# Reordering the first 28 slots of a fused thresholded attention and MoE kernel: scores first, copies a slot later, maxima two slots ahead of the gate

## The chip, the cores and the metric

The kernel runs on one core of a Trainium2 chip. A core has four compute engines with queues of their own: TensorE (PE, matmuls), VectorE (DVE), ScalarE (ACT) and GpSimd (POOL). A fifth, SyncE (SP), issues most DMA transfers. Each engine works through its instructions in the order in which the program lists them, and semaphores hold an instruction back until the data it needs are there. The metric is the device time of one launch in microseconds (us). Before the change it was 521.61 us, the median of three runs from 520.63 to 522.18. The profiled run has a span of 518.3 us, and times inside the kernel are counted from the start of that span.

## What is computed

Attention with a threshold over 8 batches of 8 heads, 576 positions and a head width of 64, and behind it a two-layer network on the 4608 x 512 result:

```python
scores = scale * q @ k.T                      # per head, 576 x 576
thresh = max(scores, -1) - tau
scores = where(scores >= thresh, scores, -1e9)
attn = exp(scores - max(scores)); attn /= sum(attn) + 1e-9
x = (attn @ v)                                # heads side by side: 4608 x 512
h = x @ w_in                                  # 512 -> 2048
out = (h * clip(h + 3, 0, 6) / 6) @ w_out     # 2048 -> 512
```

## The kernel before

**Tiles.** Four heads of a batch are a *quad*, two heads a *pair*. The 576 rows of a quad's four heads are worked off in nine *slots* of 128 rows for two heads at a time: slots 0 to 3 are the first pair's rows, 4 to 7 the second pair's, and slot 8 holds the last 64 rows of both pairs. There are 16 quads, so 144 slots, numbered n through the whole kernel. The main loop (line 527) has one pass for each slot, and the program order inside a pass is the order on each engine.

**Softmax of one slot.** `scores(n)` (line 277) multiplies on PE into PSUM. `sm_max` (294) lets DVE copy the scores to SBUF and take the row maxima, one instruction for each head (line 302), and POOL makes the bias from the maxima (305). `sm_mask` (307) rejects values under the threshold on ACT (309), and `sm_exp` (312) takes exponentials and their sum on ACT (314). `sm_recip` (316) inverts the sum on DVE, and `sm_norm` (319) multiplies on POOL (322) into `pn`, bf16. Then `pn` is transposed. In the early slots that are marked `on_chip`, PE does it two slots later (`pe_transpose`, 333) and DVE copies the result out of PSUM (338). For all others a DMA transpose does it.

**Other work on PE.** Inputs of the first two batches are transposed by PE as well (`transpose_q`, `transpose_k`, `transpose_rest`), each followed by a copy out of PSUM, which `copy_out` gives to DVE in slots 0 to 21 and to ACT later. `av_main` and `av_rest` multiply probabilities with v (346, 349) and are copied out by DVE (357, 367). The MoE's first product `mm1` (381) gives `h`. ReLU of h + 3 runs on ACT in even slots from 22 on (389) and on DVE in odd ones (391), and the *gate* on DVE (404) takes the minimum with 6 and multiplies with `h`. `mm2_part` (415) is the second product. The first MoE item is worked in slot 22 (`N1 = 22`), the first second product in slot 30.

**PSUM.** All eight banks are one tile. Scores of even slots, and of all slots to 24, lie in columns 128 to 703 and 1664 to 2239. Scores of odd slots from 25 on have a second place (`score_col`, 274). Transposes of inputs and products take banks 2 and 5 in turn (`bank()`). Bank 6 (`HB`) takes warm-up matmuls, the transposes of `pn` and `mm1`; bank 7 (`OB`) takes `mm2` and, in some odd slots, `mm1`.

**Order of a pass before the change.** In slots 1 to 21, DVE starts with the maxima of slot n+1, while ACT takes the exponentials of slot n-1 and then masks slot n. PE transposes `pn` of slot n-2, makes the products due (`multiply`), transposes inputs due in this slot (`turns`), and then makes `scores(n+2)`. DVE copies each of these results out of PSUM before the next maxima. From slot 23 on, scores of two slots are made together, at the end of each odd slot. In slot 22 the first MoE item and its ReLU come ahead of ACT's mask of that slot. `warm_up(6)`, six idle transposes, follows the scores in slots 0 to 7.

Of the kernel before, what the change touches and what calls it, by code (L numbers as in the profile page):

```python
# [20 lines left out]
def kernel(  # L21
# [17 lines left out]
    NQUAD = B * H // 4  # L39
    NSLOT = 9  # L40
    NB = 2
    N1 = 22
    N2 = 28
    HB, OB = 6, 7
# [126 lines left out]
    def start(jobs, n):  # L171
        for _ in range(min(n, len(jobs))):
            jobs.pop(0)()
# [9 lines left out]
    def warm_up(count):  # L183
        for _ in range(count):
            nc.tensor.transpose(ps[:, HB, 0:P], identf[:], identf[:])
# [30 lines left out]


    def copy_out(out, in_):
        if 0 <= now < N1:
            nc.vector.tensor_copy(out=out, in_=in_)  # L220
        else:
            nc.scalar.copy(out=out, in_=in_)  # L222
# [54 lines left out]
    def scores(n):  # L277
        quad, slot = divmod(n, NSLOT)
        w0 = 320 if first(n) else 384
        for k0, w in ((0, w0), (w0, S - w0)):  # L280
            for i in range(2 if slot == 8 else 1):
                for a in range(2):
                    pair = 2 * quad + (i if slot == 8 else slot // 4)
                    rows = slice(64 * i, 64 * i + 64) if slot == 8 else slice(0, P)
                    q0 = 512 if slot == 8 else slot % 4 * P
                    c0, kc = score_col(n, a) + k0, 64 * (1 - a) + k0
                    nc.tensor.matmul(ps_flat[rows, c0:c0 + w],  # L287
                                     qT_of(pair)[a * 64:(a + 1) * 64, q0:q0 + rows.stop - rows.start],
                                     kT_of(pair)[a * 64:(a + 1) * 64, kc:kc + w], start=True, stop=True)
# [4 lines left out]
    def sm_max(sl):  # L294
        sl.s = s_pool.tile([P, 2, S], F32, tag="s", name="s")
        sl.m = stat_pool.tile([P, 2], F32, tag="m", name="m")
        sl.bias = stat_pool.tile([P, 2], F32, tag="bias", name="bias")
        sl.rsum = stat_pool.tile([P, 2], F32, tag="rsum", name="rsum")
        sl.rinv = stat_pool.tile([P, 2], F32, tag="rinv", name="rinv")
        for i in range(2):  # L300
            c0 = score_col(sl.n, i)
            nc.vector.tensor_scalar(out=sl.s[:, i, :], in0=ps_flat[:, c0:c0 + S],  # L302
                                    scalar1=1.0, scalar2=None, op0=Alu.mult, op1=Alu.max,
                                    accum_out=sl.m[:, i:i + 1])
        nc.gpsimd.tensor_scalar(out=sl.bias[:], in0=sl.m[:], scalar1=-scale, scalar2=tau, op0=Alu.mult, op1=Alu.add)  # L305

    def sm_mask(sl, i):
# [4 lines left out]
    def sm_exp(sl, i):  # L312
        s = sl.s[:, i, :]
        nc.scalar.activation(out=s, in_=s, func=Act.Exp, accum_out=sl.rsum[:, i:i + 1])  # L314

    def sm_recip(sl):
        nc.vector.reciprocal(out=sl.rinv[:], in_=sl.rsum[:])  # L317
# [15 lines left out]
    def pe_transpose(sl):  # L333
        pb = ps_flat[:, HB * 512:HB * 512 + S].bitcast(BF16).rearrange("p (c t) -> p c t", t=P)
        pn = sl.pn[:].rearrange("p a b -> p (a b)")
        for c in range(9):
            nc.tensor.transpose(pb[:, c, :], pn[:, c * P:(c + 1) * P], identb[:])
        return lambda: nc.vector.tensor_copy(out=sl.dst, in_=pb)
# [138 lines left out]
            queue.append(sl)  # L477
    scores(0)
    sm_max(queue[0])
    scores(1)  # L480

    turns = {1: [("q", 1)], 2: [("k", 1)], 3: [("rest", 0)]}

    def turn_at(n, job, of):
        turns.setdefault(n, []).append((job, of))

    for quad in range(1, NQUAD):
        n0 = quad * NSLOT
        first_odd = n0 - 9 + quad % 2
        for i, (job, of) in enumerate((("q", 2 * quad), ("k", 2 * quad), ("rest", quad),  # L490
                                       ("q", 2 * quad + 1), ("k", 2 * quad + 1))):
            turn_at(n0 + (-5, -4, -3, 0, 1)[i] if quad < 3 else
                    first_odd + (0, 2, 3, 4, 6)[i] if quad > 3 else first_odd + (0, 2, 3, 5, 7)[i], job, of)

    products = {}
    for quad in range(NQUAD):
        p0, p1 = 2 * quad, 2 * quad + 1
        if quad < NB:
            jobs = ((8, p0, 0, 512), (12, p1, 0, 512), (13, None, 0, 0))
        else:  # L500
            jobs = [(7 - quad % 2 + 2 * i, *of) for i, of in enumerate(
                ((p0, 0, 256), (p0, 256, 256), (p1, 0, 256), (p1, 256, 256), (None, 0, 0)))]
        for after, *of in jobs:
            products.setdefault(quad * NSLOT + after, []).append((quad, *of))
# [22 lines left out]
    for n, sl in enumerate(queue):  # L527
        quad, slot = sl.quad, sl.slot
        b, g = divmod(quad, 2)
        now = n  # L530
        if slot in (0, 4):
            pts[2 * quad + slot // 4] = pt_pool.tile([P, 9, 512], BF16, tag="pT", name="pT")
        if slot == 8:
            ptr[quad] = ptr_pool.tile([P, 9, P], BF16, tag="pR", name="pR")
        for ahead in {0: (1, 2), 9: (3,), 16: (4,)}.get(n, (quad + 2,) if quad > 2 and slot == (2 if quad == 3 else 0) else ()):
            if ahead < NQUAD:
                load_quad(ahead)
        if slot == 0 and g == 1 and b + 1 < B:
            load_v(b + 1)
        for copy in last_keys:  # L540
            copy()
        last_keys = []
        if 0 < n <= N1:
            for i in range(2):
                sm_exp(prev, i)
        if n + 1 < len(queue):
            sm_max(queue[n + 1])
        even = n >= N1 and n % 2 == 0
        if n > N1:
            sm_recip(prev)  # L550
        for copy in waiting:
            copy()
        waiting = []

        if todo1:
            item, then = todo1.pop(0)
            if n == len(queue) - 2:
                second()
            h = mm1(item, 0 if n == len(queue) - 1 else OB if n > N1 and n % 2 and not pieces else HB)
            todo2.extend(then)  # L560
        else:
            item = None
        if n >= N1:
            for copy in multiply(n):
                copy()
        if item:
            mm1_gate(item, h, mm1_relu(h, on_act=even))
        copies = pe_transpose(queue[n - 2]) if n > 1 and queue[n - 2].on_chip else None
        if prev is not None and n < N1:
            sm_recip(prev)  # L570
        if copies:
            copies()
        if n != len(queue) - 2:
            second()
        if n <= N1:
            for i in range(2):
                sm_mask(sl, i)
        if n == N1:
            sm_recip(prev)
        if n >= N1:  # L580
            for i in range(2):
                sm_exp(sl, i)
            if n + 1 < len(queue):
                for i in range(2):
                    sm_mask(queue[n + 1], i)
        if n < N1:
            for copy in multiply(n):
                copy()
        if part == 3:
            waiting.append(lambda tile=(bb, mt): late.extend(mm2_out(*tile, on_act=False)))  # L590
            part = 0
        evict = []
        for job, of in turns.get(n, ()):
            if job == "k":
                (last_keys if even else evict).append(transpose_k(of))
            elif job == "q":
                if of // 2 not in qkT:
                    alloc_qk(of // 2)
                (waiting if even else evict).append(transpose_q(of))
            else:  # L600
                (last_keys if even else evict).append(transpose_rest(of, of_k=of > 0))
        for out_of_psum in evict:
            if out_of_psum:
                out_of_psum()
        if n == 0:
            warm_up(8)
        if n <= N1:
            scores(n + 2)
        elif n % 2:
            for m in (n + 3, n + 2):  # L610
                if m < len(queue):
                    scores(m)
        if n < 8:
            warm_up(6)
        if n > 0:
            sm_norm(prev)
        flush()
        if n == 0:
            start(loads, 2)
        elif n not in (4, 12, 15, 18, 21) and not 23 < n < 30 and (n < 37 or n % 2 == 0):  # L620
            start(loads, 1)
        if n < 4 or 15 < n < 20 or n > 33:
            start(vcasts, 1 if n < N1 or n % 2 else 0)
        else:
            start(casts, 2 if n in (5, 8, 11, 14) or 21 < n < 28 else 1)
        prev = sl
# [82 lines left out]
```

## Time and profile before

| what | value |
|---|---|
| median of three runs | 521.61 us |
| span of the profiled run | 518.3 us |
| busy share of the span | PE 98%, ACT 87%, DVE 85%, POOL 58% |
| chain that ended last, by engine | PE 81%, ACT 3%, DVE 2% |
| first mask on ACT (slot 0) | 10.09 us |
| mask of slot 3 / 22 / 31 begins | 18.10 / 76.52 / 104.22 us |
| start of the maxima of slot 4 / 23 on DVE | 19.50 / 75.03 us |
| first MoE matmul on PE | 74.85 us |

Busy time is what an engine worked; the rest of its time it waited. A busy share over the whole span mixes stages that have different limits, so the prediction reads the kernel in stretches, and within them the timeline of one engine. A row of a timeline gives start and length in us, the engine, the line of the kernel and the operation, the tiles it writes and reads, how many instructions are merged, and, in brackets, how long the engine stood idle before it and which work ended that idle time. Matmuls overlap and the end of each is modelled by the profiler, so starts are the safer numbers on PE.

### The profile page before, as it was taken

What the parts mean: (1) busy time and instruction counts of PE and PEld (TensorE: products, weight loads), DVE (VectorE), ACT (ScalarE), POOL (GpSimd) and SP (SyncE); (2) the same over time, 40 slices, a digit from 0 to 9 for tenths busy, and PEclk for the clock granted to TensorE, in tenths of its full rate; (3) what the DMA queues carried; (4) which work ended last, traced back from release to release, by engine and by line L of the source; (5) the groups of instructions that cost most, each with busy time, mean ns of one, the idle gap of its engine ahead of it and who ended that gap; (6) DMA issues with size and microseconds to landing.
All of it is one profiled execution on the core that took longest, in us unless ns stands there. A gap on an engine that the chain in (4) does not pass through costs nothing.

```text
span 518.3 us, 12124 instructions
## 1 busy us (share of the span) xinstructions
PE 505.9 (98%) x4145; PEld 321.1 (62%) x4145; DVE 442.6 (85%) x1124; ACT 452.1 (87%) x980; POOL 299.3 (58%) x538
## 2 busy tenths in 40 slices
PE   8999999999999999999999999999999999999997
PEld 6765556666665666666665666666665666667563
DVE  3788887998999999999999999999999999887261
ACT  3999979999999999999999999999999999987060
POOL 1778869756676666657566656657566655552000
PEclk9999999999999999999999999999999999999999
DMA  5899899989999999999979998999999997564222
GB/s 132 123 173 163 142 161 156 174 147 171 167 178 157 170 162 183 177 170 179 177 150 164 157 199 159 166 166 178 167 163 168 178 178 123 114 113 71 77 67 61
DMA packets 314094, 78.77 MB, mean 152 GB/s; under 512 B 296624, under 2 KB 309168, under 8 KB 314032
## 3 DMA queue, kind: packets, MB, share of 16 engines
q1 hardware_dynamic: 294464, 67.90, 76.0%
q0 software_dynamic: 18368, 9.71, 15.1%
q8 instruction: 32, 0.52, 0.4%
q10 hardware_dynamic: 1200, 0.39, 0.3%
q14 instruction: 30, 0.25, 0.2%
HBM read 36.70 MB, written 9.44 MB: 89 GB/s over the span
## 4 chain that ended last, share of the span: by engine, by line
PE 81%; ACT 3%; DVE 2%; POOL 0%; issue 0%; POOLq 0%
PE ps L287 25%; PE ps L415 24%; PE ps L381 21%; PE ps L346 7%; PE ps L376 3%; ACT s L314 1%; PE ps L349 1%; ACT s L309 1%; DVE g L404 1%; ACT r L389 1%; DVE s L302 0%; DVE r L391 0%; POOL pn L322 0%; PE ps L257 0%; ACT kT L222 0%; DVE xT L357 0%
## 5 line engine op out<-in xcount | busy, mean ns | idle before, releaser
L322 POOL TENSOR_SCALAR pn<-s,rinv 128x576 bf16<-128x576 f32 x288 | 210.6, 743 | 19.0 <-issue 4.5
L302 DVE TENSOR_SCALAR_CACHE_REDUCE s<-ps 128x576 f32<-128x576 f32 x288 | 205.1, 749 | 17.6 <-PE ps L287 9.0
L309 ACT ACTIVATE s<-s,bias 128x576 f32<-128x576 f32 x288 | 205.8, 763 | 6.0 <-POOL bias L305 5.7
L314 ACT ACTIVATE s<-s 128x576 f32<-128x576 f32 x288 | 192.5, 671 | 0.3
L287 PE MATMUL ps<-kT,qT 64*128 64x384 f32 (+7 forms) x1280 | 174.0, 419 | 4.7 <-DVE s L302 3.8
L287 PEld LDWEIGHTS ps<-kT,qT 64*128 64x128 f32 (+1 forms) x1280 | 103.6, 175 | 59.3 <-issue 15.8
L415 PE MATMUL ps<-w_out_sb,g 128*128 128x512 bf16 x576 | 134.1, 379 | 0.0
L381 PE MATMUL ps<-xT,w_in_sb 128*128 128x256 bf16 x1024 | 130.9, 273 | 0.2 <-DVE g L404 0.2
L381 PEld LDWEIGHTS <-w_in_sb 128*128 128x128 bf16 x1024 | 95.5, 98 | 40.0 <-issue 20.8
L305 POOL TENSOR_SCALAR bias<-m 128x2 f32<-128x2 f32 x144 | 26.9, 187 | 154.5 <-DVE rinv L317 136.6
L404 DVE SCALAR_TENSOR_TENSOR g<-r,ps 128x512 bf16<-128x512 f32 x128 | 87.9, 687 | 15.2 <-ACT r L389 11.2
L415 PEld LDWEIGHTS <-g 128*128 128x128 bf16 x576 | 56.2, 98 | 56.8 <-issue 0.4
L389 ACT ACTIVATE r<-ps,three 128x512 f32<-128x512 f32 x81 | 55.6, 687 | 27.9 <-PE ps L381 23.8
L314 ACT ACTIVATION_READ_ACCUMULATOR s<-s 128x1 f32 x288 | 54.5, 189 | 0.0
L391 DVE TENSOR_SCALAR r<-ps 128x512 f32<-128x512 f32 x63 | 42.9, 681 | 0.0
L346 PE MATMUL ps<-pT,vm 128*64 128x256 bf16 (+1 forms) x480 | 39.1, 285 | 0.0
L346 PEld LDWEIGHTS <-vm 128*64 128x64 bf16 x736 | 27.3, 110 | 16.0 <-issue 14.3
L357 DVE CAST xT<-ps 128x256 bf16<-128x256 f32 (+1 forms) x60 | 26.3, 438 | 11.8 <-PE ps L349 11.8
L423 DVE TENSOR_SCALAR osb<-ps 128x512 f32<-128x512 f32 x31 | 20.9, 673 | 8.4 <-PE ps L415 8.4
L302 DVE DVE_READ_ACCUMULATOR s<-ps 128x1 f32 x288 | 23.9, 83 | 0.0
L317 DVE RECIPROCAL rinv<-rsum 128x2 f32<-128x2 f32 x144 | 23.0, 160 | 0.6 <-ACT s L314 0.6
L143 POOL DMA_DIRECT2D vm<-in_v_dram x28 | 21.4, 765 | 0.7 <-issue 0.7
(57 smaller groups left out, 259.4 us busy)
## 6 DMA issues: line engine op xcount, KB each, us to landing
out_dram<-osb SPq DMA_DIRECT2D x31, 256.0 KB, 2.9
nq<-in_q_dram SPq DMA_DIRECT2D x96, 72.0 KB, 3.5
km<-in_k_dram SPq DMA_DIRECT2D x96, 64.0 KB, 3.2
vm<-in_v_dram POOLq DMA_DIRECT2D x24, 128.0 KB, 4.0
km<-in_k_dram SPq DMA_DIRECT2D x16, 128.0 KB, 3.6
w_in_sb<-in_moe_w_in_dram POOLq DMA_DIRECT2D x16, 128.0 KB, 3.6
w_out_sb<-in_moe_w_out_dram POOLq DMA_DIRECT2D x16, 128.0 KB, 4.1
pT<-pn SPq DMA_TRANSPOSE x117, 4.0
```

Source lines behind the costliest of these rows:

```text
L287: nc.tensor.matmul(ps_flat[rows, c0:c0 + w], qT_of(pair)[a * 64:(a + 1) * 64, q0:q0 + rows.stop - rows.start], kT_of(pair)[a * 64:(a + 1) ...
L302: nc.vector.tensor_scalar(out=sl.s[:, i, :], in0=ps_flat[:, c0:c0 + S], scalar1=1.0, scalar2=None, op0=Alu.mult, op1=Alu.max, accum_out=sl ...
L305: nc.gpsimd.tensor_scalar(out=sl.bias[:], in0=sl.m[:], scalar1=-scale, scalar2=tau, op0=Alu.mult, op1=Alu.add)
L309: nc.scalar.activation(out=s, in_=s, func=Act.Prelu, bias=sl.bias[:, i:i + 1], scale=scale, alpha=REJECT)
L314: nc.scalar.activation(out=s, in_=s, func=Act.Exp, accum_out=sl.rsum[:, i:i + 1])
L322: nc.gpsimd.tensor_scalar(out=pn[:, i, :], in0=sl.s[:, i, :], scalar1=sl.rinv[:, i:i + 1], scalar2=1.0, op0=Alu.mult, op1=Alu.mult)
L346: nc.tensor.matmul(pb[a * 64:(a + 1) * 64, :], vm[:, 2 * hp + a, c * D:(c + 1) * D], pT[:, 5 * a + c, cols], start=(c == 0), stop=False)
L381: nc.tensor.matmul(ps[:, hb, n * 256:(n + 1) * 256], w_in_sb[:, ki, (ni + n) * P:(ni + n + 1) * P], xT[b][:, ki, c0:c0 + 256], start=(ki = ...
L389: nc.scalar.activation(out=r, in_=hps, func=Act.Relu, bias=three[:])
L391: nc.vector.tensor_scalar(out=r, in0=hps, scalar1=3.0, scalar2=0.0, op0=Alu.add, op1=Alu.max)
L404: nc.vector.scalar_tensor_tensor(out=out, in0=r, scalar=6.0, in1=hps, op0=Alu.min, op1=Alu.mult)
L415: nc.tensor.matmul(o_ps[0], gbuf[:, ni, mt * P:(mt + 1) * P], w_out_sb[:, ni, :], start=(ni == 0), stop=(ni == NI - 1))
```

## The change

In slots 3 to 21 it puts `scores(n+2)` ahead of all other work of PE in its pass, and does the copies of everything else that PE has made (transposed probabilities, products, transposed inputs) a slot later, behind the next maxima and the reciprocal. This is meant to let PE make scores as soon as the maxima have freed their place, with DVE copying meanwhile. The transposes of the first two batches' inputs are dated anew, the second pairs' sooner, so that fewer copies fall into one slot. For the same reason the last products of quads 0 and 1 move by a slot or two. Loads of quad 1 are all issued in slot 0, and warm-ups stay only in slots 0 to 3 and 6.

At slot 22 the masks of slots 22 and 23 and the exponentials of slot 22 come ahead of the first ReLU. In the even slots 22 to 28, the exponentials come ahead of the ReLU, and DVE takes the maxima of slot n+2 as well, ahead of the gate, so that the scores made at the end of the odd slot find both places free. The bias on POOL becomes a function of its own (`sm_bias`) and stays in its slot.

```diff
+    N0 = 3
     def copy_out(out, in_):
-        if 0 <= now < N1:
+        if 0 <= now <= N1:
...
-            turn_at(n0 + (-5, -4, -3, 0, 1)[i] if quad < 3 else
+            turn_at(n0 + ((-5, -5, -4, -2, -1) if quad == 1 else (-6, -5, -4, -2, -1))[i] if quad < 3 else
...
-            jobs = ((8, p0, 0, 512), (12, p1, 0, 512), (13, None, 0, 0))
+            jobs = ((8, p0, 0, 512), (13 - 2 * quad, p1, 0, 512), (15 - 3 * quad, None, 0, 0))
...
         if n + 1 < len(queue):
-            sm_max(queue[n + 1])
+            if n <= N1 or n > N2 + 1 or n % 2 == 0:
+                sm_max(queue[n + 1])
+            sm_bias(queue[n + 1])
         even = n >= N1 and n % 2 == 0
-        if n > N1:
+        if n >= N0:
             sm_recip(prev)
         for copy in waiting:
             copy()
         waiting = []
+        if N0 <= n <= N1:
+            scores(n + 2)
+            if n in (3, 6):
+                warm_up(6)
+        if even and n <= N2:
+            sm_max(queue[n + 2])
+        if n == N1:
+            for i in range(2):
+                sm_mask(sl, i)
+        exp_first = even and n <= N2
+        if exp_first:
+            for i in range(2):
+                sm_exp(sl, i)
+        if n == N1:
+            for i in range(2):
+                sm_mask(queue[n + 1], i)
-        if todo1:
+        if todo1 and n >= N1:
...
-        copies = pe_transpose(queue[n - 2]) if n > 1 and queue[n - 2].on_chip else None
-        if prev is not None and n < N1:
+        if n > 1 and queue[n - 2].on_chip:
+            waiting.append(pe_transpose(queue[n - 2]))
+        if prev is not None and n < N0:
             sm_recip(prev)
...
         if n < N1:
-            for copy in multiply(n):
-                copy()
+            waiting.extend(multiply(n))
...
+        if N0 <= n < N1:
+            waiting.extend(evict)
+            evict = []
...
-        if n <= N1:
+        if n < N0:
             scores(n + 2)
-        elif n % 2:
+            warm_up(6)
+        elif n > N1 and n % 2:
...
-        if n < 8:
-            warm_up(6)
...
         if n == 0:
-            start(loads, 2)
+            start(loads, 5)
```

More of the change, by code (lines that the diff above doesn't have):

```diff
@@ L304, in sm_max, with sm_bias @@
                                     accum_out=sl.m[:, i:i + 1])
+    def sm_bias(sl):
         nc.gpsimd.tensor_scalar(out=sl.bias[:], in0=sl.m[:], scalar1=-scale, scalar2=tau, op0=Alu.mult, op1=Alu.add)
@@ L479 @@
     sm_max(queue[0])
+    sm_bias(queue[0])
     scores(1)
@@ L567 @@
             mm1_gate(item, h, mm1_relu(h, on_act=even))
-        copies = pe_transpose(queue[n - 2]) if n > 1 and queue[n - 2].on_chip else None
-        if prev is not None and n < N1:
+        if n > 1 and queue[n - 2].on_chip:
+            waiting.append(pe_transpose(queue[n - 2]))
+        if prev is not None and n < N0:
             sm_recip(prev)
-        if copies:
-            copies()
+            for copy in waiting:
+                copy()
+            waiting = []
         if n != len(queue) - 2:
             second()
-        if n <= N1:
+        if n < N1:
             for i in range(2):
                 sm_mask(sl, i)
-        if n == N1:
-            sm_recip(prev)
         if n >= N1:
-            for i in range(2):
-                sm_exp(sl, i)
-            if n + 1 < len(queue):
+            if not exp_first:
+                for i in range(2):
+                    sm_exp(sl, i)
+            if n != N1 and n + 1 < len(queue):
                 for i in range(2):
@@ L601 @@
                 (last_keys if even else evict).append(transpose_rest(of, of_k=of > 0))
+        evict = [out_of_psum for out_of_psum in evict if out_of_psum]
+        if N0 <= n < N1:
+            waiting.extend(evict)
+            evict = []
         for out_of_psum in evict:
-            if out_of_psum:
-                out_of_psum()
+            out_of_psum()
         if n == 0:
             warm_up(8)
-        if n <= N1:
+        if n < N0:
             scores(n + 2)
-        elif n % 2:
+            warm_up(6)
+        elif n > N1 and n % 2:
             for m in (n + 3, n + 2):
```

## The prediction

> **What bounds the kernel now.** I first read the slices of the page: TensorE (PE) is 90% busy or more from the first slice to the last but one, so the page alone cannot say what a change at the start is worth. I then cut the span at events of the slots: ScalarE (ACT) begins the mask of slot 3 at 18.10 us, ends the exponentials of slot 21 at 72.61, begins the mask of slot 22 at 76.52 and that of slot 31 at 104.22. Busy time by stretch:
>
> ```profile
> core 0: us, PE busy (x) PEld busy (x) DVE busy (x) ACT busy (x) POOL busy (x), PEclk, DMA share, GB/s
> 18.10:72.60 54.50, 51.32 (x420) 33.05 (x422) 46.01 (x128) 51.81 (x116) 43.88 (x81) 1.00 1.01 161
> 72.60:76.50 3.90, 3.90 (x48) 2.48 (x44) 3.05 (x8) 0.67 (x3) 1.93 (x3) 1.00 0.94 125
> 76.50:104.20 27.70, 25.55 (x196) 16.94 (x195) 23.94 (x63) 27.58 (x62) 23.17 (x43) 1.00 1.16 171
> 104.20:484.00 379.80, 379.60 (x3197) 239.03 (x3195) 349.21 (x883) 350.80 (x768) 225.43 (x399) 1.00 0.97 160
> ```
>
> From 104 us on PE has no gap, so whatever moves the start of that stretch moves the end by as much. Before it ACT is the fullest engine: 27.58 of 27.70 in slots 22 to 30, but 0.67 of 3.90 at the turn, and some loss in slots 3 to 21. Undisturbed, a slot costs ACT 2.665 us (masks at 12.77, 15.43, 18.10). The 19 slots from 18.10 to 72.61 took 54.51 against 19 x 2.665 = 50.64: 3.87 lost. The turn, in the timeline of ACT:
>
> ```profile
> 72.52 0.19 ACT L314 ACTIVATION_READ_ACCUMULATOR s<-s 128x1 f32 x1
> 75.93 0.69 ACT L389 ACTIVATE r<-ps,three 128x512 f32<-128x512 f32 x1 [3.23 <-PE ps L381]
> 76.52 1.43 ACT L309 ACTIVATE s<-s,bias 128x576 f32<-128x576 f32 x2
> ```
>
> The ReLU of the first MoE item stands ahead of slot 22's mask and waits 3.23 us for its matmul. Why that is late, and what costs the 3.87, shows in PE and VectorE (DVE) of slot 21:
>
> ```profile
> 70.83 0.40 PE L337 MATMUL ps<-identb,pn 128*128 128x128 bf16 x4
> 71.50 0.45 PE L337 MATMUL ps<-identb,pn 128*128 128x128 bf16 x5 [0.27 <-POOL pn L322]
> 71.89 1.05 PE L346 MATMUL ps<-pT,vm 128*64 128x512 bf16 x8
> 72.78 0.38 PE L349 MATMUL ps<-pT,vr 128*64 128x512 bf16 x2
> 73.09 0.66 PE L232 MATMUL ps<-identf,km 128*128 128x128 f32 x4
> 73.67 1.24 PE L287 MATMUL ps<-kT,qT 64*128 64x384 f32 x8
> ```
>
> ```profile
> 70.71 0.76 DVE L302 TENSOR_SCALAR_CACHE_REDUCE s<-ps 128x576 f32<-128x576 f32 x1 [0.37 <-issue]
> ...
> 73.20 0.69 DVE L357 CAST xT<-ps 128x512 bf16<-128x512 f32 x1 [0.32 <-PE ps L349]
> 73.81 0.68 DVE L220 COPY kT<-ps 128x512 f32<-128x512 f32 x1
> 75.03 0.76 DVE L302 TENSOR_SCALAR_CACHE_REDUCE s<-ps 128x576 f32<-128x576 f32 x1 [0.54 <-issue]
> ```
>
> Scores come last on PE, behind transposes and products; the next maxima wait for them. One period of maxima was 4.32 us here (70.71 to 75.03). Over slots 3 to 21 maxima start at 19.50 ... 75.03: 19 periods, mean 2.92. The shortest is 2.53 (68.18 to 70.71), where scores followed the maxima at once; the longest are those with products or three copies: 3.48, 3.73, 3.29, 4.32.
>
> **What the Trainium skill says.** "PSUM — Partial Sum Buffer", section "Engine vs sequencer instructions": ACT, DVE and GpSimd queues are strict FIFO, and matmuls start in program order. The trace agrees: slot 22's bias was written by 72.44, yet its mask stood behind the ReLU until 76.52. The same page, section "PSUM bank collisions raise a hardware error": accesses to a bank must be kept apart by semaphores, so scores wait for the maxima that read their banks; here PE weight loads of scores waited 11.0 us for DVE up to 112 us. "TensorE: Matmul & The Clock Gate", part 1: about 3.4 us of idleness can halve the PE clock. That bears on the warm-ups removed; PEclk is 1.00 in 18 to 104 us, though slots 8 to 21 have none.
>
> **The change, part by part.**
>
> 1. *Scores ahead of the other PE work, copies a slot later (slots 3 to 21).* Nothing is added. One period becomes the longest of: the loop maxima, scores, maxima (2.54, as 42.20 to 44.75 and 68.18 to 70.71 show); the DVE work; what PE still has queued. DVE start to start: maxima 1.36, reciprocal 0.08, transposed probabilities 0.65, a q, k or product copy 0.60.
>    - Seven slots (3, 7, 10, 11, 12, 16, 19) have at most one such copy: 2.54 each, 17.78.
>    - Five (5, 8, 13, 17, 20) have two: 1.36 + 0.08 + 0.65 + 0.60 = 2.69, 13.45.
>    - Four (9, 14, 18, 21) follow a product. Scores end 2.45 after the maxima begin; product 1.20 and a key transpose 0.58 then end at 4.23, the next scores 1.2 later, the next maxima start near 5.5; less the 2.69 of the period before, 2.80 each, 11.20.
>    - Two (6, 15) carry the ninth slot's doubled scores: 2.81 (27.86 to 30.67), 5.62.
>    - Slot 4: 2.58, warm-up and transposes behind scores.
>
>    Sum 50.63 against 55.53: maxima of slot 23 start at 19.50 + 50.63 = 70.1, not 75.03. ACT alone would reach slot 22's mask at 21.26 (slot 4) + 18 x 2.665 = 69.2; DVE permits it at 67.3 + 1.76 = 69.1 (maxima 2.8 earlier; 1.76 is 19.50 to 21.26). Two chains so alike delay each other; I add 0.4, an estimate: **69.6**, 6.9 before 76.52.
> 2. *Later keys, rest and product of quads 0 and 1; earlier second pairs.* The count of instructions stays. They are spread so that no slot has three copies before slot 22; the last rest-product (0.45 of PE) leaves slot 22 for slot 21. In the sums above.
> 3. *Warm-ups dropped in slots 4, 5, 7.* Bursts of some 0.7 us, not on the new chain. I take zero; the bad end is 1 us if the clock fell.
> 4. *Five loads at once in slot 0 instead of two.* The queue had issued its seven by 9.8 us and then stood until 16.6 behind the first DMA transpose; six more issues of 1.2 us fill that gap. DMA share was 0.39 in 10 to 15 us. Zero.
> 5. *Turn at slot 22.* Masks and exponentials of 22 and the mask of 23 go ahead of the ReLU, so the 3.23 wait is hidden behind 4 us of ACT work. The ReLU (0.67 with its gap) now comes after: the gain at the mask of slot 31 is 6.9 - 0.7 = **6.2**.
> 6. *Maxima of slots 24, 26, 28, 30 a slot earlier, exponentials ahead of the ReLU.* No work is added. At odd slots scores no longer wait for DVE: PE loses the 1.00, 0.17 and 0.98 idle at 85.99, 92.03, 98.40 and 3 x 0.74 inside the blocks (2.88 against 2.14), 4.37 in all. But ACT is full there, so this pays only in letting PE keep up. The gate stands behind two more maxima (2.72) on DVE; behind it wait the bank's next MoE matmul and the reciprocal for GpSimd. The ReLU that it needs is itself two exponentials later, so I take zero.
>
> PE after: scores of 24 end near 72.5, 24.5 us of work follow to the scores of 33 and 34 (28.94 from 76.63 to 105.57, less 4.37), so 97.0 without waits. ACT sets it: ReLU of slot 30 at 102.30 - 6.2 = 96.1, ReLU and gate 1.3, matmul 1.0, product 0.7: 99.1 to 99.4 against 105.57. So 6.2: 521.6 - 6.2 = **515.4**.
>
> **The rivals.**
> - *The start improves by half.* A copy held a slot longer also holds its bank; if PE then waits, periods average 2.85: 19 x 2.85 = 54.2, slot 22's mask at 72.6, gain 3.9 - 0.7 = 3.3, 518.3. For it: DVE slots filled to 2.69. Against: a bank is needed again only after the next scores, about 2.45 into the slot, and is free by 2.1 or 2.7.
> - *Nothing arrives.* DMA (share 1.16 in slots 22 to 30) delivers transposed probabilities or output weights no sooner, PE waits there instead: 521. Against: no long DMA wait on PE stands in the table of waits.
> - *Slower.* The gate slips by 1.36 in four even slots and PE waits each time for its bank (+5.4), and only the 3.2 of the turn are won: 523.8. For: gate and bank chain through DVE, which is 86% busy there. Against: PE keeps 4.4 us of slack.
>
> **How the numbers follow.** Forecast 0.62, half 0.23, nothing 0.06, slower 0.09. The best end is ACT without any loss (7.1) and PE's 1.3 of slack: 513.2. The range, 513.4 to 518.9, holds forecast and half; outside lie the last two cases and a little of each end. Faster by over 0.3% (below 520.0): 0.86; within: 0.05; slower: 0.09.
>
> **What would show it.** Maxima periods in slots 3 to 21 at a mean near 2.67, none over 3; no wait over 0.6 of ACT for PE at slot 22, mask of 22 near 69.6, of 31 near 98; PE without gaps from about 98; clock 1.00. Wrong if matmuls wait for evictions of banks 2, 5 or 6, if maxima wait for GpSimd's normalisation to free a score tile, or if PE idles after 100 us.

## The result, and the profile after

The changed kernel takes 516.88 us (516.83 to 517.00, three runs) against 521.61: a ratio of 0.9912, with a 95% interval of 0.9888 to 0.9936. A second group of runs gave 516.82 against 520.61, ratio 0.9924 (0.9912 to 0.9936), so the gain is nearer 4 us than 5. The direction and the range of the prediction hold; its 515.4 was 1.5 us too low. Part of that nearness is luck: the forecast was a gain of 6.2 us counted from 521.61, and those three runs lie 1.0 us above the 520.6 of all later groups. The gain itself came to about six tenths of the 6.2 (3.6 to 3.8 us).

The same cut into stretches, at the masks of slots 3, 22 and 31, in the changed kernel (columns: stretch, length, then busy time and instruction count of PE, PEld, DVE, ACT and POOL, granted clock, DMA share, GB/s):

```profile
18.44:71.70 53.26, 51.48 (x401) 31.47 (x403) 45.75 (x128) 51.47 (x116) 45.20 (x82) 1.00 1.04 160
71.70:101.00 29.30, 27.92 (x245) 18.40 (x242) 26.65 (x70) 28.17 (x62) 23.80 (x44) 1.00 1.10 167
101.00:480.80 379.80, 379.55 (x3195) 238.87 (x3193) 349.15 (x883) 350.88 (x768) 226.47 (x399) 1.00 1.02 160
```

The third stretch is cut to the same length, 379.80 us, in both kernels; TensorE is busy for 379.55 us of it here and for 379.60 before. From the mask of slot 31 to the end of the span it is 414.1 us in both (101.00 to 515.1, and 104.22 to 518.3), so whatever the change earned it had earned by the mask of slot 31. Up to slot 22 it took 53.26 instead of 58.42 (18.10 to 76.52): 5.2 won. From slot 22 to 31 it took 29.30 instead of 27.70: 1.6 given back, where the forecast allowed 0.7.

All this happens behind a start that varies by up to a microsecond between profiled runs, in transposes and loads that the change leaves alone: the first mask began at 10.09 before, at 10.44 here, and at 11.07 in another run of the same changed kernel. I therefore compare kernels by the time from the first mask to that of slot 31. It was 94.13 before and 90.56 here, and 90.57 in the other run: 3.57 won, the same to 0.01 in the two profiled runs of the changed kernel.

The turn at slot 22 in the timeline of ScalarE (start, length, engine, line, operation, tiles; in brackets idle time before it and what ended it):

```profile
71.70 1.44 ACT L312 ACTIVATE s<-s,bias 128x576 f32<-128x576 f32 x2 [0.70 <-POOL bias L308]
...
74.38 1.43 ACT L312 ACTIVATE s<-s,bias 128x576 f32<-128x576 f32 x2
75.92 0.69 ACT L392 ACTIVATE r<-ps,three 128x512 f32<-128x512 f32 x1
77.56 0.53 ACT L223 COPY kT<-ps 64x128 f32<-64x128 f32 x2 [0.95 <-DVE qT L266]
...
79.47 1.43 ACT L312 ACTIVATE s<-s,bias 128x576 f32<-128x576 f32 x2
```

The wait of 3.23 us for the first MoE matmul is gone, since two masks and an exponential pair now cover it. Two smaller waits have appeared: 0.70 for the bias of slot 22, and 0.95 at the key copies of slot 23, which ran at 80.51 without a wait before. Neither stood in the prediction. The first has its cause on GpSimd, in its timeline:

```profile
68.17 1.47 POOL L325 TENSOR_SCALAR pn<-s,rinv 128x576 bf16<-128x576 f32 x2
69.58 1.26 POOL L127 DMA_DIRECT2D kr<-in_k_dram  x2
70.82 0.58 POOL L169 DMA_DIRECT2D w_out_sb<-in_moe_w_out_dram  x1
71.48 0.18 POOL L308 TENSOR_SCALAR bias<-m 128x2 f32<-128x2 f32 x1
```

With all of quad 1's loads issued in slot 0, every later load job moved up. The last key rows of quad 4 are issued by GpSimd, and this job came from slot 22 to slot 20, where its 1.26 us stand between the normalisation and the bias of slot 22. Before, it ran at 79.02 to 80.29.

Why the periods of the maxima are still longer than forecast shows on TensorE in slot 8:

```profile
34.51 1.56 PE L288 MATMUL ps<-kT,qT 64*128 64x384 f32 x8
36.00 1.05 PE L349 MATMUL ps<-pT,vm 128*64 128x512 bf16 x8
36.89 0.38 PE L352 MATMUL ps<-pT,vr 128*64 128x512 bf16 x2
37.20 0.66 PE L233 MATMUL ps<-identf,km 128*128 128x128 f32 x4
37.79 1.24 PE L288 MATMUL ps<-kT,qT 64*128 64x384 f32 x8
```

Scores do come first (34.51), but a product and a key transpose behind them occupy TensorE to 37.79. The next scores could have begun a microsecond earlier, as VectorE had read the first of their two places by 36.8. The next maxima began at 39.14, 3.11 after the last. The periods of slots 3 to 21 now are 2.54 where the loop alone counts, 2.69 with two copies, 3.11 to 3.14 in the four slots behind a product, and 2.88 to 2.90 in slots 4, 6 and 15. Their sum is 52.33 and their mean 2.75, against 55.53 and 2.92 before and a forecast of 50.63.

### The profile page after: what moved, and what is told of

Read it like the earlier page. It is cut to its first block, busy times and chain, and to the rows that moved or that the text cites. A ratio compares the mean times of both kernels' runs of the same rounds, so it can differ in the third digit from the quotient of the medians.

```text
span 515.1 us, 12094 instructions
## 1 busy us (share of the span) xinstructions
PE 504.9 (98%) x4127; PEld 318.6 (62%) x4127; DVE 441.9 (86%) x1124; ACT 451.8 (88%) x980; POOL 300.4 (58%) x538
## 4 chain that ended last, share of the span: by engine, by line
PE 79%; ACT 5%; DVE 2%; issue 0%
PE ps L288 24%; PE ps L418 24%; PE ps L384 20%; PE ps L349 7%; PE ps L379 3%; ACT s L317 2%; ACT s L312 2%; PE ps L352 1%; ACT r L392 1%; DVE g L407 1%; DVE r L394 0%; PE ps L340 0%; DVE s L303 0%; ACT kT L223 0%; PE ps L258 0%
```

## The experiments

For each kernel, times in us from mask to mask as above, with the median of its timed runs. The ratio is to the kernel before, run beside it (520.6 in each of the three groups); as recorded, it can differ by 0.001 from the quotient of the two medians.

| kernel | mask 0 to 22 | 22 to 31 | 0 to 31 | median | ratio (95% interval) |
|---|---|---|---|---|---|
| before | 66.43 | 27.70 | 94.13 | 520.6 | 1 |
| changed, second group | 61.26 | 29.31 | 90.57 | 516.82 | 0.9924 (0.9912 to 0.9936) |
| start only | 66.08 | 27.70 | 93.78 | 520.37 | 0.9990 (0.9982 to 0.9999) |
| turn only | 62.52 | 31.24 | 93.76 | 520.41 | 0.9990 (0.9980 to 1.0000) |
| no maxima ahead | 61.25 | 31.05 | 92.30 | 518.76 | 0.9958 (0.9943 to 0.9974) |
| keys on VectorE | 61.26 | 28.05 | 89.31 | 515.06 | 0.9892 (0.9879 to 0.9905) |
| rest load on SyncE | 60.48 | 30.09 | 90.57 | 516.82 | 0.9925 (0.9914 to 0.9937) |
| keys, load and ReLU | 60.48 | 29.30 | 89.78 | 516.42 | 0.9916 (0.9905 to 0.9928) |
| second keys later | 60.38 | 29.29 | 89.67 | 516.37 | 0.9907 (0.9890 to 0.9923) |
| all three | 59.67 | 28.74 | 88.41 | 514.01 | 0.9876 (0.9857 to 0.9895) |
| old warm-ups and loads | 61.10 | 30.08 | 91.18 | 517.96 | 0.9942 (0.9923 to 0.9960) |

Two more, with copies in the same slot and with the old dates, are told below.

### Do the two parts add up?

The first kernel has the new slots 3 to 21 and the old order from slot 22 on, with one exception: in slot 22 TensorE still makes the scores of slot 24 ahead of the first MoE matmul, as in the changed kernel:

```diff
-            if n <= N1 or n > N2 + 1 or n % 2 == 0:
-                sm_max(queue[n + 1])
+            sm_max(queue[n + 1])
...
-        if even and n <= N2:
-            sm_max(queue[n + 2])
-        if n == N1:
-            for i in range(2):
-                sm_mask(sl, i)
-        exp_first = even and n <= N2
+        exp_first = False
...
-        if n == N1:
-            for i in range(2):
-                sm_mask(queue[n + 1], i)
...
-        if n < N1:
+        if n <= N1:
             for i in range(2):
                 sm_mask(sl, i)
...
-            if n != N1 and n + 1 < len(queue):
+            if n + 1 < len(queue):
```

> Only slots 3 to 21 are changed (scores first, copies a slot later, new dates, loads and warm-ups); slot 22 and the even slots to 28 keep the old order, the ReLU ahead of the mask of slot 22, maxima one slot ahead. Theory A (the turn at slot 22 binds what the start wins): the first MoE matmul stands behind the scores of slot 24 and ended near 75.9 us in the changed kernel, so the ReLU and the mask of slot 22 behind it come near 76.5 as before; gain under 1 us, 520.7 to 521.8. Theory B (the start pays by itself and the turn is a second, separate gain): mask of slot 22 near 73, gain 3 us or more, 518.6 or less.

The second has the old slots 3 to 21 and the new ones from 22 on:

```diff
-    N0 = 3
+    N0 = 22
...
-            turn_at(n0 + ((-5, -5, -4, -2, -1) if quad == 1 else (-6, -5, -4, -2, -1))[i] if quad < 3 else
+            turn_at(n0 + (-5, -4, -3, 0, 1)[i] if quad < 3 else
...
-            jobs = ((8, p0, 0, 512), (13 - 2 * quad, p1, 0, 512), (15 - 3 * quad, None, 0, 0))
+            jobs = ((8, p0, 0, 512), (12, p1, 0, 512), (13, None, 0, 0))
...
-            if n in (3, 6):
-                warm_up(6)
...
-            waiting.extend(multiply(n))
+            for copy in multiply(n):
+                copy()
...
-            warm_up(6)
+            if n < 8:
+                warm_up(6)
...
-            start(loads, 5)
+            start(loads, 2)
```

> Only slots 22 to 28 are changed, slots 3 to 21 keep the old order, dates, loads and warm-ups. Theory A (the two parts need each other): the mask of slot 22 can start near 72.7 as its bias is there at 72.4, but the maxima of slot 23 start near 75.0 as before and the mask of slot 23 waits for them to 76.8; of the 3.2 us about 1 is left, less the ReLU moved behind: 520.5 to 521.8. Theory B (two separate gains): 3.2 less 0.7, so 519.1 or less.

Both came as theory A said, with medians 0.1 to 0.3 below its ranges. Alone, the parts win 0.35 and 0.37 of the 94.13; together 3.57. The timelines show why. First ScalarE and then TensorE in the kernel with the start only, then ScalarE in the one with the turn only:

```profile
75.86 0.69 ACT L392 ACTIVATE r<-ps,three 128x512 f32<-128x512 f32 x1 [4.92 <-PE ps L384]
76.45 1.43 ACT L312 ACTIVATE s<-s,bias 128x576 f32<-128x576 f32 x2
```

```profile
73.56 1.28 PE L288 MATMUL ps<-kT,qT 64*128 64x384 f32 x8
74.78 1.05 PE L384 MATMUL ps<-xT,w_in_sb 128*128 128x256 bf16 x8
```

```profile
72.44 1.43 ACT L312 ACTIVATE s<-s,bias 128x576 f32<-128x576 f32 x2
...
76.62 1.44 ACT L312 ACTIVATE s<-s,bias 128x576 f32<-128x576 f32 x2 [1.43 <-POOL bias L308]
```

With the start alone, the scores and masks up to slot 21 run ahead, but the first matmul stands behind slot 24's scores and starts at 74.78, about as late as the 74.85 before; the ReLU waits 4.92 us for it with slot 22's mask behind it. With the turn alone, slot 22's mask is off at 72.44, but the maxima of slot 23 are as late as before (74.85), and its mask waits for the bias. Each part removes one of two waits that end at about the same time. Some of this depends on where the order of slot 22 is counted. With the matmul ahead of slot 24's scores, as before the change, it could have begun near 73.56, and the start alone would have won up to 1.2 us more. That is an estimate from the two TensorE rows above; such a kernel was not run.

### Are the maxima of two slots ahead worth anything?

```diff
-            if n <= N1 or n > N2 + 1 or n % 2 == 0:
-                sm_max(queue[n + 1])
+            sm_max(queue[n + 1])
...
-        if even and n <= N2:
-            sm_max(queue[n + 2])
...
-        exp_first = even and n <= N2
+        exp_first = n == N1
```

> The changed kernel without the maxima of two slots ahead and without exponentials ahead of the ReLU in slots 24, 26 and 28; the turn at slot 22 stays. Theory A (ScalarE is full from slot 22 to 30, so a better feed of TensorE is worth nothing): 516.6 to 517.4, mask of slot 31 within 0.4 us of the changed kernel's 101.0. Theory B (without them TensorE falls behind at the odd slots again): its idle of 1.0, 0.2 and 1.0 us returns and the time rises by 1.5 to 3, 518.4 to 520. Theory C (the gate behind two maxima costs): faster, 516 or less.

Theory B: 1.7 us longer from slot 22 to 31, 518.76. Step 6 took them at zero. The idle times that theory B named came back on TensorE, 1.28, 0.17 and 0.97 us ahead of the scores at the end of slots 23, 27 and 29, but only the first is followed by a wait of ScalarE. From the mask of slot 24 to that of slot 25 it is 4.82 us instead of 3.36, so most of the loss falls there. VectorE, TensorE and ScalarE in this kernel:

```profile
76.55 0.69 DVE L407 SCALAR_TENSOR_TENSOR g<-r,ps 128x512 bf16<-128x512 f32 x1 [1.50 <-ACT r L392]
77.15 0.28 DVE L266 COPY qT<-ps 128x128 f32<-128x128 f32 x1
77.35 0.75 DVE L303 TENSOR_SCALAR_CACHE_REDUCE s<-ps 128x576 f32<-128x576 f32 x1
```

```profile
78.16 3.04 PE L288 MATMUL ps<-kT,qT 64*64 64x384 f32 x24 [1.28 <-DVE s L303]
```

```profile
82.28 0.69 ACT L392 ACTIVATE r<-ps,three 128x512 f32<-128x512 f32 x1 [1.49 <-PE ps L384]
```

The gate waits 1.50 us for the ReLU, which cannot start before the first matmul has ended, and holds the maxima of slot 24 behind it to 77.35. (With the start only, where the ReLU stands ahead of the mask, the gate waits 1.50 us too.) In the changed kernel these start at 75.06 and fill the wait. Here TensorE's scores then wait 1.28 us for them, the matmul of slot 24 behind the scores is late, and slot 24's ReLU on ScalarE waits 1.49 for that. So what was undone is worth something mainly at the turn, where the maxima fill VectorE's wait, and little in the later slots. The edit also puts slot 24's ReLU back ahead of its exponentials, which could have covered part of the 1.49 us. What each of the two is worth was not run separately.

### Is it the order on TensorE, or the copies a slot later?

```diff
             waiting.append(pe_transpose(queue[n - 2]))
+            if n >= N0:
+                waiting.pop()()
...
-            waiting.extend(multiply(n))
+            for copy in multiply(n):
+                copy()
...
-        if N0 <= n < N1:
-            waiting.extend(evict)
-            evict = []
```

> The changed kernel with scores first in slots 3 to 21, but every copy out of PSUM in the slot of its transpose or product. Theory A (the overlap of copies with the next scores is what shortens the period): VectorE waits in each slot until TensorE has done scores, transposes and products, periods of the maxima of 3.3 to 5 us, mean 3.7 against 2.75, so about 18 us longer: 530 to 538. Theory B (the order on TensorE alone is what counts): mean period under 2.85, 516.5 to 518.5.

574.91 us, a ratio of 1.102 (1.099 to 1.106), 37 us above the top of theory A's range; the mean period is 5.76 us where theory A had 3.7. In its table of waits for 20 to 130 us (us in total, times, longest), VectorE stands 30.4 us for the transposed probabilities alone, which now come behind the scores:

```profile
DVE pT L341 <- PE ps L340: 30.4, 11, 3.4
```

The rest of the loss I had not foreseen. The page's clock row, a digit for each fortieth of the span, in tenths of full speed:

```profile
PEclk9966676667999999999999999999999999999999
```

TensorE ran at six to seven tenths through the slow stretch. The long periods came first: that of slot 3, from 19.97 to 24.92 us, took 4.95 us instead of 2.55 while the clock was still 1.00; it was 0.81 from 25.0 to 27.5 us and 0.51 from 27.5 to 30.0. So theory A holds at the full clock as well: scores first do not pay without the later copies. How much of the rest is the slower clock cannot be read from this kernel. Later copies with the old order on TensorE were not run.

### What are the new dates worth?

```diff
-            turn_at(n0 + ((-5, -5, -4, -2, -1) if quad == 1 else (-6, -5, -4, -2, -1))[i] if quad < 3 else
+            turn_at(n0 + (-5, -4, -3, 0, 1)[i] if quad < 3 else
...
-            jobs = ((8, p0, 0, 512), (13 - 2 * quad, p1, 0, 512), (15 - 3 * quad, None, 0, 0))
+            jobs = ((8, p0, 0, 512), (12, p1, 0, 512), (13, None, 0, 0))
```

> The changed kernel with the old dates of transposes and products of quads 0 to 2 (quad 1: 4, 5, 6, 9, 10; quad 2: 13, 14, 15, 18, 19; products after slots 12, 13, 21 and 22). Theory A (the order alone, with copies a slot later, shortens the periods; the dates smooth): slots with three copies or a product near 3.3, the first matmul's input copied in slot 22, 0.4 to 1.5 slower than the changed kernel, 517.2 to 518.4. Theory B (the new dates are most of the gain): 519.5 or more.

Theory B, and by more than it asked: 521.56, slower than before the change (1.0021, 1.0011 to 1.0031). With the old dates a second pair's keys are transposed one slot before the scores that need them are due. Copied a slot later, they are copied in the slot of those scores, behind VectorE's maxima, and the scores wait. On TensorE this shows in slots 11 and 20:

```profile
45.15 1.24 PE L288 MATMUL ps<-kT,qT 64*128 64x384 f32 x8 [1.72 <-DVE kT L221]
...
74.44 1.24 PE L288 MATMUL ps<-kT,qT 64*128 64x384 f32 x8 [1.28 <-DVE kT L221]
```

Two shorter waits of this kind, 0.52 and 0.53 us, are for the keys of the last rows. The profiled execution, at 524.06, was the slowest of the twenty, with a clock of 0.66 from 60 to 70 us, so these waits are a sample and not a sum of the loss. The lower clock is not what loses the gain: the six executions with a mean clock of 1.000 took 520.33 to 521.47. The dates of the products were undone together with those of the transposes, and what each is worth was not run.

### What are warm-ups and loads worth?

```diff
-            if n in (3, 6):
+            if n < 8:
                 warm_up(6)
...
-            start(loads, 5)
+            start(loads, 2)
```

> The changed kernel with the six warm-up transposes in each of slots 0 to 7 and with two loads in slot 0 instead of five, as before the change. Theory A (both are free, as the prediction took them): within 0.4 of the changed kernel, 516.4 to 517.3, clock 1.00 in both. Theory B (warm-ups ahead of transposes lengthen the periods of slots 4, 5 and 7): those periods 0.3 to 0.7 longer, 517.4 or more.

0.6 us longer to the mask of slot 31, and 1.1 in the medians (of two groups of runs): theory B in its direction, though the periods that grew are not the ones it named. The period of slot 8 is 3.22 instead of 2.69 and that of slot 5 is 2.85 instead of 2.62 (slot 9's is shorter, 2.96 for 3.11); all periods of slots 3 to 21 together are 0.62 longer. The warm-ups of slots 7 and 4, 0.7 us each, stand ahead of the next slot's matmuls on TensorE. Loads and warm-ups were undone together; I put the longer periods down to the warm-ups because they lie next to them, which is argued and not shown. (The load that delays slot 22's bias makes no difference at slot 31, as a kernel below shows.) The clock was 1.00 from 18 to 75 us in both kernels.

### Where the missing gain was

Five kernels take away the waits found above, one at a time and together. Key copies of slot 23 on VectorE:

```diff
-        if 0 <= now <= N1:
+        if 0 <= now <= N1 + 1:
```

> The changed kernel, but the two copies of the last keys at the start of slot 23 run on VectorE instead of ScalarE. In the changed kernel ScalarE stands idle 0.95 us there, because the same PSUM bank is first read by VectorE, whose copy is queued behind the gate of slot 22, and then copies for 0.53. Theory A (ScalarE sets the pace from slot 22 to 30): mask of slot 24 about 1.5 earlier, gain 1.2 to 1.5, 515.3 to 515.8. Theory B (VectorE sets it by then): the copies only move, the maxima of slot 25 come later and the gain is under 0.4.

1.26 us less from slot 22 to 31: theory A, though the median, 515.06, is 0.2 under its range. Both copies read one PSUM bank, and VectorE's stands behind the gate (in the changed kernel the gate starts at 76.64, VectorE's copy at 77.24, ScalarE's at 77.56), so ScalarE had waited for the gate that waits for its own ReLU. The edit takes the 0.53 us of copying off ScalarE as well as the 0.95 us of waiting, so the 1.26 is not the price of the wait alone. In this kernel the next mask follows the ReLU and the exponentials (rows left out) without a gap:

```profile
75.50 0.69 ACT L392 ACTIVATE r<-ps,three 128x512 f32<-128x512 f32 x1
77.41 1.43 ACT L312 ACTIVATE s<-s,bias 128x576 f32<-128x576 f32 x2
```

The last key rows of quad 4 loaded by SyncE:

```diff
-                    (nc.sync if b < NB else nc.gpsimd).dma_start(out=dst[64 * n:64 * n + 64, :].rearrange("p (h d) -> p h d", h=2),
+                    (nc.sync if quad < 5 else nc.gpsimd).dma_start(out=dst[64 * n:64 * n + 64, :].rearrange("p (h d) -> p h d", h=2),
```

> The changed kernel, but the two loads of the last key rows of quad 4 are issued by the SyncE queue, not by GpSimd, where they take 1.26 us in slot 20 and stand ahead of the bias of slot 22. Theory A (slot 22's mask is then only earlier than its ReLU, which waits for the matmul): mask of slot 22 about 0.7 earlier, mask of slot 24 unmoved, no gain, 516.6 to 517.1. Theory B (each delay of ScalarE counts): 0.7 faster, 516.2.

Theory A: slot 22's mask 0.78 earlier, slot 31's unmoved to the hundredth. The ReLU cannot pass the first matmul, so the 0.70 wait was free in the changed kernel. Both edits and the first ReLU on VectorE:

```diff
-            mm1_gate(item, h, mm1_relu(h, on_act=even))
+            mm1_gate(item, h, mm1_relu(h, on_act=even and n > N1))
```

> The changed kernel with the key copies of slot 23 on VectorE, the loads of quad 4's last keys on SyncE, and the first ReLU (slot 22) on VectorE too. ScalarE then has no wait for the first matmul at all. Theory A (ScalarE sets the pace): mask of slot 24 near 77, gain 2 to 2.5 against the changed kernel, 514.4 to 515. Theory B (VectorE, which takes 1.1 us more, sets it from the maxima of slot 25 on): gain as with the keys alone, 515.3 to 515.9.

Neither theory had the size: 0.8 better than the changed kernel, and 0.5 worse than the keys alone. The ReLU takes 0.7 of VectorE; the maxima of slot 25 start 5.01 us after those of slot 24 (75.43, 80.44) instead of 4.53 with the keys alone (74.63, 79.16), and slot 25's mask waits 0.84 for its bias. What ScalarE was relieved of, VectorE lacked.

The second pairs' keys a slot later, out of the slots that have a product:

```diff
-            turn_at(n0 + ((-5, -5, -4, -2, -1) if quad == 1 else (-6, -5, -4, -2, -1))[i] if quad < 3 else
+            turn_at(n0 + ((-5, -5, -4, -2, 0) if quad == 1 else (-6, -5, -4, -2, 0))[i] if quad < 3 else
```

> The changed kernel, but the second pairs' keys of quads 1 and 2 are transposed one slot later (slots 9 and 18), so that they no longer share a slot with an attention product (8 and 17). Theory A (a product and a key transpose behind the scores keep TensorE 1.8 us, which makes the next period 3.11 instead of 2.54 to 2.69): the periods of slots 9 and 18 fall to 2.55 to 2.75, the maxima of slot 23 start 0.7 to 1.0 earlier, gain 0.5 to 0.9 against the changed kernel. Theory B (ScalarE and GpSimd set the pace of slots 3 to 21, not this chain): periods fall there and grow elsewhere, gain under 0.2.

Theory A: the periods of slots 9 and 18 fall from 3.11 to 2.53, those of slots 10 and 19 grow from 2.54 to 2.69 with the copy, and 0.90 is won by the mask of slot 31 (0.45 in the medians, which come from two groups of runs). Last, these second keys, the key copies and the load together:

> The second keys a slot later, the key copies of slot 23 on VectorE, and the last key rows of quad 4 loaded by SyncE. Theory A (three waits in one line: scores of slot 23, bias of slot 22, key copies of slot 23): from the start of slot 0's mask to that of slot 31 1.8 to 2.3 us less than the changed kernel's 90.6, 514.5 to 515.0. Theory B (only the keys on VectorE count): as they alone, 89.3 and 515.1 to 515.6.

2.16 us less than the changed kernel at the mask of slot 31, within theory A's 1.8 to 2.3, and a median of 514.01, 0.5 under its range and better than the second keys or the key copies alone. But the size is that of two waits and not of three: 0.90 for the second keys and 1.26 for the key copies are 2.16 already, and the load adds nothing that shows. It brings slot 22's mask 0.7 us earlier, to 69.70, and the ReLU then waits 0.54 us for the first matmul (rows of exponentials left out):

```profile
72.64 1.44 ACT L312 ACTIVATE s<-s,bias 128x576 f32<-128x576 f32 x2 [0.17 <-POOL bias L308]
74.62 0.69 ACT L392 ACTIVATE r<-ps,three 128x512 f32<-128x512 f32 x1 [0.54 <-PE ps L384]
76.54 1.43 ACT L312 ACTIVATE s<-s,bias 128x576 f32<-128x576 f32 x2
```

## Why the prediction was right, and where it was short

- *The number.* The forecast gain was 6.2 us, 6.9 at slot 22's mask less 0.7 at the turn. Like for like it was 3.57: 5.17 at slot 22's mask, less 1.6 from there to slot 31. That 516.88 lies as near to 515.4 as it does owes 1.0 us to the high median before the change. The last kernel, with two of the waits away, wins 5.72 (88.41 for 94.13).
- *A gain before 104 us moves the end by as much.* Right: 414.1 us from slot 31's mask to the end in both kernels.
- *Step 1, scores first and copies later.* Right in kind: no period over 3.14, where there had been 3.48, 3.73 and 4.32. The mean is 2.75 instead of the 2.67 forecast, and four periods are over 3, where the prediction had none. The term for the four slots behind a product was mis-sized, 2.80 against 3.11 to 3.14, which makes 1.3 of the 1.7 us by which the sum fell short; slot 4 (2.88 for 2.58) makes 0.3. The product's slot itself runs 0.2 us later than I had it, and the scores then begin late and run to their end before the maxima can start. Moving the key transpose out of the product's slot took 0.58 off the period behind it in two of the four cases (the slot after that grew by 0.15), so the term is shown for these two.
- *The 69.6 for slot 22's mask.* It came at 71.70, 71.36 on the old start. About 0.7 of the 1.8 is the bias behind GpSimd's loads, from step 4, which I had taken at zero from the queue of slot 0 alone, without asking where the later loads would land. It cost nothing in the end. Most of the rest is the periods behind products: with the second keys moved and the load on SyncE, in the last kernel, the mask comes 59.67 us after the first one, which is 69.76 on the old start.
- *Step 2, new dates.* "In the sums above" hid their weight: without the new dates nothing is won (521.56 against 520.56).
- *Step 3, warm-ups at zero.* The dropped ones gave about 0.6, if it was they and not the loads; the clock stayed at 1.00.
- *Step 5, the turn.* The 0.7 for the ReLU agrees with the 0.69 us that it takes. What the step missed is 0.95 at the key copies of slot 23: I counted ScalarE's own work and not what shares a bank with it behind VectorE's gate. With these copies on VectorE the wait is gone and 1.26 us is won.
- *Step 6 at zero.* Wrong: undoing it costs 1.7. The zero rested on ScalarE being full from slot 22 on; it left out that VectorE stands 1.50 us at the first gate with the maxima of slot 24 behind it, unless these go ahead.
- *The parts in a sum.* Start and turn are no sum: 0.35 and 0.37 alone, 3.57 together. The later mends are one: 0.90 and 1.26 alone, 2.16 together.
- *The rivals.* The time lies midway between forecast and "half", and the gain of 3.57 is close to the 3.3 of "half"; but the banks held longer, which "half" gave as its cause, show no wait of TensorE: between the masks of slots 3 and 22 its matmuls waited 1.5 us for maxima and, as in the kernel before, 0.9 us for one copy of keys. The gate bound once before slot 31: TensorE stood idle for 0.56 us up to 100.55 us, the idleness after 100 us that the prediction had named as a sign against itself.

## What to carry to other kernels

When two chains are about equally late, removing the waits of one can buy almost nothing: look for what will end last afterwards, and change both. In a strict queue, an instruction that waits charges its wait to all behind it, so when a producer moves back, fill the consumer's queue ahead of the wait with work that is ready. And when work is spread over slots, ask for every issue and copy that moves along which queue it lands in, and what shares its bank.

## What the runs showed of the hardware

In the kernel with copies in the same slot, TensorE's clock fell to means of 0.59 to 0.75 in the 20-us stretches from 20 to 140 us, although TensorE counted as busy for 77% of that time (92.45 of 120 us), no gap between its matmuls was longer than 1.92 us, and the longest wait of a weight load was 2.3. The changed kernel, busy for 116.83 us in the same stretches, kept a clock of 1.00. The Trainium skill, "TensorE: Matmul & The Clock Gate", Part 1, ties the lower clock to an idle window of some 3.4 us; under "A second HAM failure mode: psum-queue depth-cycling" the same page has a kernel whose clock swings because TensorE idles for short times often. This trace agrees with the second: gaps well under the window, often repeated, went with the low clock. That the gaps are its cause was not tried separately.
